# The decay rows of the first pair of heads: written in place by two engines, or transferred

## The chip, the cores and the metric

The kernel runs on one core of a Trainium2 chip. The metric is the device time of one execution in microseconds (us). Each core has five engines: TensorE (PE, with its weight loads shown apart as PEld), VectorE (DVE), ScalarE (ACT), GpSimd (POOL) and SyncE (SP, which here issues the transfers).

## The reference

The program is causal attention with a decay, for 8 batches of 8 heads (576 tokens, head size 64), and behind it a gated mixing network over the tokens. Cut to what matters:

```python
scores = scale * np.matmul(q, k.transpose(0, 1, 3, 2))
log_f = np.log(np.clip(f, 0.0001, 1.0))
cum = np.cumsum(log_f, axis=-1)
decay = cum[:, :, :, None] - cum[:, :, None, :]
scores = np.where(causal, -1000000000.0, scores + decay)
attn = softmax(scores)                       # 1e-9 added to the sum
x = heads side by side of np.matmul(attn, v)
h = np.maximum(x @ w_in, 0.0)
u, v = h[..., :d_ff // 2], h[..., d_ff // 2:]
gated = u * (w_spatial @ normalised(v) + b_spatial)
out = gated @ w_out
```

## The kernel before

The heads are worked in 32 pairs. `attention` runs over the four pairs of a batch, `moe` over the batches; an outer loop takes steps of both in turn by fixed costs, and a scheduler then orders each engine's instructions for the whole program. A call `after(i, mark)` asks it to put `i` behind an earlier instruction; it adds no wait on the chip.

For a head, `scores` makes four tiles of 128 queries (128, 256, 384 and 512 keys) and `scores_tail` the last 64 queries of both heads. TensorE multiplies queries by keys into PSUM (three buffers at the start), VectorE adds the mask `zm` and takes the row extremum (L287, L308), ScalarE takes the exponential and its sum (L289, L313), POOL scales by the reciprocal sum (L297, L320). `tt[0]`, `tt[1]` and `tl` hold the results. Then come transposes (L343, L356) and the product with the values (`attend`).

The decay is part of the score product. An operand tile `tf` has 66 partitions: 64 of the head's size and two rows of decay. Its first 640 columns are queries, the last 576 keys. In the key columns the two rows are cum and 8; in the query columns they are -8 and cum; in query columns that belong to the other head of the pair they are 0. Their product adds 8 times the difference of the cumulative sums, and VectorE's step scales by -0.125.

`decay_rows` makes these rows once for all 64 heads, one head to a partition, in `r0`: constants by `decay_consts` (POOL memsets L82 and L83, VectorE memsets L85), the gates `f` by a transfer (L95), clamp (L100), Ln (L101), the running sum (L103), then `queries_rows` copies the sums into the query columns (L89 on VectorE, L91 on ScalarE). The one-element exponential in L102 makes ScalarE load its table early. `prep` loads a head's operand for the first four pairs: one transfer of queries and keys (L241) and one of the two decay rows from `r0` (L242). Later pairs read their rows from `rows_d` in memory, which `split_rows` fills: `rt` holds the sums in two parts (ScalarE casts L110, L89, L91 and a POOL subtraction L111), and one transfer stores it (L113).

While the first pair's operands are made, TensorE runs 30 products of zeros (`zm`), so that its clock is at full speed when the scores begin.

Weights come in 64-bit form by transfers at L135 and are converted by `conv64` (ScalarE L144, VectorE L145 to L151, POOL L153 and L155), in turn with the attention of the first batches. SP issues all loads from one queue, in order; an issue that waits holds those behind it.

Of the kernel before, what the change touches and what calls it, by code (L numbers as in the profile page):

```python
# [8 lines left out]
F32 = mybir.dt.float32  # L9
F32R = mybir.dt.float32r  # L10
BF16 = mybir.dt.bfloat16
U32 = mybir.dt.uint32
AF = mybir.ActivationFunctionType
ALU = mybir.AluOpType
# [8 lines left out]
S = 576  # L23
D = 64
NB = 4
TL = 512
# [3 lines left out]
QK = 640 + S  # L30
# [3 lines left out]
def f32(ap):  # L34
    return ap.bitcast(F32)
# [3 lines left out]
def attn_gmlp_kernel(ctx: ExitStack, tc: tile.TileContext, qk, v, f, w_in, w_sp, b_sp, w_out, out):  # L39
# [11 lines left out]
    cst = ctx.enter_context(tc.tile_pool(name="cst", bufs=1))  # L51
    wk = ctx.enter_context(tc.tile_pool(name="wk", bufs=1))
# [4 lines left out]
    V, A, G, T, SY = nc.vector, nc.scalar, nc.gpsimd, nc.tensor, nc.sync  # L57


    ident = cst.tile([128, 128], F32, name="ident")  # L60
    make_identity(nc, ident)

    zm = cst.tile([128, 928], BF16, name="zm")
    G.memset(zm, 0.0)
# [6 lines left out]
    lnc = cst.tile([128, 3], F32, name="lnc")  # L71
# [7 lines left out]

    def decay_consts(r, rows):  # L80
        r = f32(r)
        G.memset(r[:, 0:rows, 0:640], -8.0)  # L82
        G.memset(r[:, rows:2 * rows, 640:QK], 8.0)  # L83
        for p0, h in ((0, 0), (32, 1)):
            V.memset(r[p0:p0 + 32, :, S - 64 * h:640 - 64 * h], 0.0)  # L85

    def queries_rows(r, rows, copy, copy_tail):
        r_ = f32(r)
        copy(r[:, rows:2 * rows, 0:TL], r_[:, 0:rows, 640:640 + TL])  # L89
        for p0, h in ((0, 0), (32, 1)):  # L90
            copy_tail(r[p0:p0 + 32, rows:2 * rows, TL + 64 * h:S + 64 * h], r_[p0:p0 + 32, 0:rows, 640 + TL:QK])  # L91

    def decay_rows():
        ft = wk.tile([64, S], F32, name="ft", tag="vt")
        SY.dma_start(out=ft, in_=f)  # L95
        ones = wk.tile([64, S], F32, name="ones", tag="xl", bufs=5)
        V.memset(ones, 1.0)
        r0 = cst.tile([64, 2, QK], F32, name="r0", tag="el")
        decay_consts(r0[:], 1)
        V.tensor_scalar(out=ft, in0=ft, scalar1=1.0e-4, scalar2=1.0, op0=ALU.max, op1=ALU.min)  # L100
        A.activation(ft, ft, AF.Ln)  # L101
        A.activation(lnc[0:1, 2:3], ft[0:1, 0:1], AF.Exp)  # L102
        V.tensor_tensor_scan(out=r0[:, 0, 640:QK], data0=ones, data1=ft, initial=0.0, op0=ALU.mult, op1=ALU.add)  # L103
        queries_rows(r0[:], 1, V.tensor_copy, A.copy)
        return r0

    def split_rows(ws, r0):
        rt = ws.tile([64, 4, QK], F32R, name="rt", bufs=1)
        decay_consts(rt[:], 2)
        A.copy(rt[:, 0, 640:QK], r0[:, 0, 640:QK])  # L110
        G.tensor_tensor(out=rt[:, 1, 640:QK], in0=r0[:, 0, 640:QK], in1=f32(rt[:, 0, 640:QK]), op=ALU.subtract)  # L111
        queries_rows(rt[:], 2, A.copy, A.copy)
        after(SY.dma_start(out=rows_d[:], in_=f32(rt[:])), ("exp", 0, 1, 0))  # L113

    last = {}
# [11 lines left out]
    def after(i, mark):  # L127
        if mark in last:
            tc.add_manual_dep(i.ins, last[mark].ins.name, mybir.DependencyInfo(
                mybir.DependencyClass.NoSync, mybir.DependencyReason.DATA), reason="order")  # L130
# [71 lines left out]
                    SY.dma_start(out=f32(sptb[64 + r:65 + r, :]), in_=f32(bs[r][:]))  # L202
            yield 1000

    tt = [cst.tile([128, 1280], F32, name=f"tt{h}") for h in range(2)]
    tl = cst.tile([128, 640], F32, name="tl")
    G.memset(tl[:, S:640], 0.0)
    ET = {"f": cst.tile([128, 2, 1600], F32, name="ef", tag="eh")}
# [3 lines left out]
    def mm(o, l, r, st, sp):  # L212
        last['mm'] = T.matmul(o, l, r, start=st, stop=sp)  # L213
        return last['mm']
# [6 lines left out]
    vts, tab, parts, r0s = {}, {}, {}, []  # L221
# [14 lines left out]
    def prep(P, h):  # L236

        p = slice(64 * h, 64 * h + 64)
        if P < NQ:
            ta = wk.tile([66, QK], F32, name="tf", tag="ta" if P % 2 == 0 else "tb", bufs=2)  # L240
            after(SY.dma_start(out=ta[0:64, :], in_=qk[P, p, :]), ("dma", 0, 1))  # L241
            last['dma', P, h] = SY.dma_start(out=ta[64:66, :], in_=r0s[0][32 * h + P:32 * h + P + 1])  # L242
            tab[P, h] = (ta,)
            return
        hi, lo = parts[P]
        ta = wk.tile([128, QK], F32R, name="ta", tag="ta", bufs=2)
        tb = wk.tile([128, QK], F32R, name="tb", tag="tb", bufs=2)
        SY.dma_start(out=f32(ta[0:64, :]), in_=hi[p, :])
        SY.dma_start(out=f32(ta[64:128, 0:640]), in_=lo[p, 0:640])
        SY.dma_start(out=f32(ta[64:128, 640:QK]), in_=hi[p, 640:QK])  # L250
        SY.dma_start(out=f32(tb[0:64, 0:640]), in_=hi[p, 0:640])
        SY.dma_start(out=f32(tb[0:64, 640:QK]), in_=lo[p, 640:QK])
        after(SY.dma_start(out=f32(tb[64:68, :]), in_=rows_v[:, P, h, :]), ("exp", P - 1, 0, 0))
        tab[P, h] = (ta, tb)
# [144 lines left out]
    def attention(b, ws=None):  # L399
        for P in range(b * PPB, (b + 1) * PPB):  # L400
            if P == 0:
                r0s.append(decay_rows())
                for h in range(2):
                    prep(0, h)

                warm = ps_a.tile([128, 512], F32, name="x0")
                for _ in range(30):
                    mm(warm, zm[:, 0:128], zm[:, 0:512], True, True)
                yield from scores(0, 0)
                yield from scores_tail(0)  # L410
                yield from scores(0, 1)
                for _ in range(6):
                    after(T.matmul(warm, zm[:, 0:128], zm[:, 0:512], start=True, stop=True), 'mm')
            nxt = P + 1 < NPAIR
            prep_v(P)
            if nxt:
                prep(P + 1, 0)
                prep(P + 1, 1)
            if P == 0:
                split_rows(ws, r0s[0])  # L420
            yield from transposes(P, 0)
            if nxt:
                yield from scores(P + 1, 0)
            yield from transposes_tail(P)
            if P + 2 < NPAIR:
                split(P + 2)
            if nxt:
                yield from scores_tail(P + 1)
            xh = wk.tile([128, 640], F32R, name="xh", tag="xh", bufs=5)
            xl = wk.tile([128, S], F32R, name="xl", tag="xl", bufs=5)  # L430
            yield from attend(P, 0, xh, xl)
            yield from transposes(P, 1)
            if nxt:
                yield from scores(P + 1, 1)
            yield from attend(P, 1, xh, xl)
            A.copy(xh[:, S:640], f32(xl[:, TL:S]))
            xs[P] = (xh, xl)
# [210 lines left out]
```

## Time and profile before

| what | value |
|---|---|
| median of 3 runs | 809.53 us (809.02 to 810.04) |
| profiled execution | 809.19 us |
| its span, first to last instruction | 807.4 us |
| mean granted TensorE clock | 0.991 |
| PE, DVE, ACT, POOL busy | 97%, 68%, 66%, 59% of the span |

A row of the timeline has the start and duration in us, the engine, the line, the operation, what it writes and reads, and in brackets the idle time before it and what ended that. The chain of work that ended last follows the end back through whatever released each step. SPq rows are issues of transfers, not their duration; landings have no rows.

### The profile page before, as it was taken

The page shows a single profiled execution, that of the slowest core. Times are in us where ns is not written, and L with a number is a line of the kernel's source. Part 1 is how long each engine was busy: PE and PEld are TensorE (multiplying, and loading weights), DVE is VectorE, ACT ScalarE, POOL GpSimd, SP SyncE. Part 2 cuts the span into 40 slices and gives each one's busy share as a digit, 9 for nine tenths or more (in the row PEclk, how much of TensorE's full clock was granted, in tenths as well). Part 3 has the DMA queues.
Part 4 walks back from the last instruction along what each step waited for, and adds up shares of the span by engine and source line. Part 5 has one row for each costly group of instructions (what it writes and reads, how often), then busy time and mean ns, then how long its engine had stood idle before and what let it go on. Part 6 is the DMA issues. An engine that isn't in the chain of part 4 may idle for free.

```text
span 807.4 us, 15507 instructions
## 1 busy us (share of the span) xinstructions
PE 786.1 (97%) x4989; PEld 704.5 (87%) x4990; DVE 550.9 (68%) x1658; ACT 536.2 (66%) x1416; POOL 479.0 (59%) x660
## 2 busy tenths in 40 slices
PE   9998989999999999999999999999999999999997
PEld 4676768998999879998899989999899988999996
DVE  5989696766756568675867668666777757665421
ACT  6768557666767578675877668577777757664431
POOL 5879697565646566554766647456675537543241
PEclk9999999999999999999999999999999999999999
DMA  6866535564465553566545644555553655330001
GB/s 175 257 228 157 150 91 140 133 166 123 97 143 134 145 153 83 130 163 162 134 115 139 161 119 120 143 136 142 145 143 106 156 148 133 74 78 14 27 1 66
DMA packets 40179, 103.49 MB, mean 128 GB/s; under 512 B 6833, under 2 KB 6833, under 8 KB 40034
## 3 DMA queue, kind: packets, MB, share of 16 engines
q1 hardware_dynamic: 39778, 101.98, 48.8%
q8 instruction: 40, 0.66, 0.3%
q10 hardware_dynamic: 320, 0.52, 0.2%
q14 instruction: 41, 0.34, 0.1%
HBM read 39.41 MB, written 10.68 MB: 62 GB/s over the span
## 4 chain that ended last, share of the span: by engine, by line
PE 85%; POOL 4%; DVE 4%; DMA 2%; ACT 2%; issue 1%; SPq 0%; POOLq 0%; ACTq 0%; DVEq 0%
PE ps L213 46%; PE sc L213 15%; PE x L213 12%; PE tp L343 7%; PE tp L213 2%; PE tp L356 2%; DMA w<-in_dram 2%; POOL tt L297 1%; DVE tt L287 1%; DVE vx L481 1%; POOL w L153 1%; DMA out_dram<-o 1%; POOL win L155 1%; ACT tt L289 0%; DVE wa L151 0%
## 5 line engine op out<-in xcount | busy, mean ns | idle before, releaser
L297 POOL TENSOR_SCALAR tt<-tt,sm 128x128 f32<-128x128 f32 (+3 forms) x256 | 141.2, 570 | 116.5 <-DVE sm L293 67.8
L287 DVE CUSTOM_DVE_ANT_0 tt<-sc,zm 128x128 f32<-128x128 f32 (+3 forms) x256 | 122.4, 486 | 109.1 <-PE tp L343 77.8
L332 ACT CAST eh<-tp 128x512 fp32r<-128x512 f32 (+1 forms) x270 | 111.4, 425 | 82.1 <-PE tp L343 51.3
L289 ACT ACTIVATE tt<-tt,nm 128x128 f32<-128x128 f32 (+3 forms) x256 | 144.4, 565 | 24.8 <-DVE nm L287 23.6
L333 DVE TENSOR_TENSOR el<-tp,eh 128x512 fp32r<-128x512 f32 (+1 forms) x270 | 127.4, 485 | 20.2 <-ACT eh L332 17.9
L343 PE MATMUL tp<-ident,tt 128*128 128x128 f32 x640 | 113.3, 279 | 4.0 <-POOL tt L297 1.8
L213 PE MATMUL sc<-ta 128*128 128x128 f32 (+1 forms) x336 | 108.8, 329 | 2.3 <-DVE nm L287 1.9
L213 PE MATMUL sc<-tb 68*128 68x128 f32 (+1 forms) x336 | 105.7, 319 | 0.0
L213 PE MATMUL x<-eh,vt 128*128 128x320 f32 (+4 forms) x378 | 103.4, 285 | 1.8 <-POOL vt L264 1.8
L213 PE MATMUL ps<-xh,win 128*128 128x256 f32 (+1 forms) x464 | 99.5, 303 | 2.1 <-DVE vx L475 2.1
L529 POOL TENSOR_TENSOR gl<-u,gh 128x256 fp32r<-128x256 f32 x64 | 47.2, 738 | 81.2 <-ACT gh L528 81.0
L213 PE MATMUL ps<-win,xh 128*128 128x512 f32 x296 | 91.9, 403 | 0.5 <-ACT o L554 0.4
L233 POOL TENSOR_TENSOR lo<-raw,hi 128x640 fp32r<-128x640 f32 (+1 forms) x56 | 83.7, 1515 | 14.6 <-ACT hi L231 14.4
L213 PE MATMUL x<-el,vt 128*128 128x256 f32 x324 | 91.3, 305 | 0.0
L343 PEld LDWEIGHTS tp<-ident,tt 128*128 128x128 f32 x640 | 77.1, 142 | 16.1 <-POOL tt L297 4.2
L213 PEld LDWEIGHTS ps<-xh,win 128*128 128x128 f32 x464 | 76.3, 191 | 3.5 <-DVE vx L475 1.9
L213 PEld LDWEIGHTS x<-eh,vt 128*128 128x128 f32 x378 | 71.4, 189 | 4.5 <-POOL vt L264 2.7
L213 PE MATMUL ps<-sph,vnh 128*128 128x256 f32 (+1 forms) x240 | 73.3, 306 | 0.2 <-ACT o L554 0.2
L391 ACT CAST xh<-x 64x256 fp32r<-64x256 f32 (+1 forms) x128 | 50.1, 394 | 33.6 <-PE x L213 31.4
L213 PE MATMUL ps<-sph,vnl 128*128 128x256 f32 (+1 forms) x240 | 71.7, 299 | 0.0
L213 PEld LDWEIGHTS sc<-ta 128*128 128x128 f32 x336 | 64.4, 192 | 7.9 <-DVE nm L287 3.2
L213 PE MATMUL ps<-spl,vnh 128*128 128x256 f32 (+1 forms) x240 | 71.2, 297 | 0.0
(173 smaller groups left out, 1916.6 us busy)
## 6 DMA issues: line engine op xcount, KB each, us to landing
raw<-in_dram SPq DMA_DIRECT2D x28, 608.0 KB
ta<-hi SPq DMA_DIRECT2D x56, 304.0 KB
vraw<-in_dram SPq DMA_DIRECT2D x32, 320.0 KB
ta<-lo SPq DMA_DIRECT2D x56, 160.0 KB
tb<-hi SPq DMA_DIRECT2D x56, 160.0 KB
out_dram<-o SPq DMA_DIRECT2D x32, 256.0 KB
ta<-hi SPq DMA_DIRECT2D x56, 144.0 KB
tb<-lo SPq DMA_DIRECT2D x56, 144.0 KB
```

The lines of the kernel that those rows point to most:

```text
L153: G.tensor_tensor(out=wf, in0=wf, in1=af, op=ALU.add)
L213: last['mm'] = T.matmul(o, l, r, start=st, stop=sp)
L233: G.tensor_tensor(out=lo[:, c], in0=raw[:, c], in1=f32(hi[:, c]), op=ALU.subtract)
L287: V.tensor_tensor_reduce(out=t, in0=sc[:, 0:n], in1=zm[:, 640 - n:640], scale=-0.125, scalar=3.0e38, op0=ALU.add, op1=ALU.min, accum_out=n ...
L289: last["exp"] = last["exp", P, h, i] = A.activation(t, t, AF.Exp, bias=nm[:, i:i + 1], scale=-1.0, accum_out=se[:, i, 0:1])
L297: G.tensor_scalar(out=t, in0=t, scalar1=sm[:, i:i + 1], scalar2=1.0, op0=ALU.mult, op1=ALU.mult)
L332: A.copy(h_ap, ps)
L333: V.tensor_tensor(out=l_ap, in0=ps, in1=f32(h_ap), op=ALU.subtract)
L343: T.transpose(out=tp[:, (i - c) * 128:(i - c + 1) * 128], in_=tt[h][:, TOFF[i] + 128 * c:TOFF[i] + 128 * c + 128], identity=ident)
L356: T.transpose(out=tp[:, j * 128:(j + 1) * 128], in_=tl[:, c * 128:(c + 1) * 128], identity=ident)
L391: last[P, h] = A.copy(hi, ps[m0:m0 + 64, 0:n])
L529: G.tensor_tensor(out=gl[j][:, 0:256], in0=g[:, 0:256], in1=f32(gh[j][:, 0:256]), op=ALU.subtract)
```

## The change

For the first pair alone, the two decay rows of each head are no longer transferred from `r0`. The gates are read a second time (`ft` has 128 partitions now), so that partitions 64 to 95 all hold the gates of head 0 of the pair and 96 to 127 those of head 1. The running sums of a head therefore stand in partitions 64 and 65 or 96 and 97 too, and `first_rows` writes the operand's two partitions from them: each row is the sums times a 0 or 1 taken from the identity matrix, plus or minus an 8 or 0 taken from `id8`. ScalarE writes the key columns, VectorE the query columns; small VectorE memsets write the zeros.

Around it, `queries_rows` for `r0` is called after the first four score tiles. The casts for `rt` get a mark behind the first head's last exponential, and the constants' memsets one behind the last of the new VectorE operations. The warming products are 18 and read zeros that VectorE writes into `tt[1]`. The mark `("dma", 0, 1)`, which the loads of other pairs and of the first weights are put behind, is now a VectorE instruction.

```diff
+    tt = [cst.tile([128, 1280], F32, name=f"tt{h}") for h in range(2)]
+    V.memset(tt[1][:, 0:320], 0.0)
+    zz = tt[1][:, 0:320].bitcast(BF16)
...
+    id8 = cst.tile([128, 64], F32, name="id8")
+    V.tensor_scalar(out=id8, in0=ident[:, 64:128], scalar1=8.0, scalar2=1.0, op0=ALU.mult, op1=ALU.mult)
...
-        G.memset(r[:, 0:rows, 0:640], -8.0)
-        G.memset(r[:, rows:2 * rows, 640:QK], 8.0)
+        after(G.memset(r[:, 0:rows, 0:640], -8.0), ("dma", 0, 1))
+        after(G.memset(r[:, rows:2 * rows, 640:QK], 8.0), ("dma", 0, 1))
...
-        ft = wk.tile([64, S], F32, name="ft", tag="vt")
-        SY.dma_start(out=ft, in_=f)
+        ft = wk.tile([128, S], F32, name="ft", tag="vt")
+        SY.dma_start(out=ft[64:128, :], in_=bass.AP(tensor=f.tensor, offset=f.offset, ap=[[32 * S, 2], [0, 32], [1, S]]))
+        SY.dma_start(out=ft[0:64, :], in_=f)
...
-        queries_rows(r0[:], 1, V.tensor_copy, A.copy)
         return r0
+
+    def first_rows(r, h):
+        g = slice(64 + 32 * h, 66 + 32 * h)
+        c = r0s[0][g, 0, 640:QK]
+        k, q = 32 * h, 32 * h + 1
+        ik, iq = (ident[g, 64 + n:65 + n] for n in (k, q))
+        bk, bq = (id8[g, n:n + 1] for n in (k, q))
+        A.activation(r[:, 640:QK], c, AF.Identity, bias=bq, scale=ik)
+        for a, n, o in ((0, S, 0),) if h == 0 else ((0, TL, 0), (TL, S - TL, 64)):
+            i = V.tensor_scalar(out=r[:, a + o:a + o + n], in0=c[:, a:a + n], scalar1=iq, scalar2=bk, op0=ALU.mult, op1=ALU.subtract)
+        return i
...
-        A.copy(rt[:, 0, 640:QK], r0[:, 0, 640:QK])
-        G.tensor_tensor(out=rt[:, 1, 640:QK], in0=r0[:, 0, 640:QK], in1=f32(rt[:, 0, 640:QK]), op=ALU.subtract)
+        after(A.copy(rt[:, 0, 640:QK], r0[0:64, 0, 640:QK]), ("exp", 0, 0, 3))
+        G.tensor_tensor(out=rt[:, 1, 640:QK], in0=r0[0:64, 0, 640:QK], in1=f32(rt[:, 0, 640:QK]), op=ALU.subtract)
...
-            last['dma', P, h] = SY.dma_start(out=ta[64:66, :], in_=r0s[0][32 * h + P:32 * h + P + 1])
+            if P == 0:
+                V.memset(ta[64:66, S - 64 * h:640 - 64 * h], 0.0)
+                last['dma', P, h] = first_rows(ta[64:66], h)
+            else:
+                last['dma', P, h] = SY.dma_start(out=ta[64:66, :], in_=r0s[0][32 * h + P:32 * h + P + 1])
...
-                for _ in range(30):
-                    mm(warm, zm[:, 0:128], zm[:, 0:512], True, True)
+                for _ in range(18):
+                    mm(warm, zz[:, 0:128], zz[:, 128:640], True, True)
                 yield from scores(0, 0)
+                queries_rows(r0s[0][0:64], 1, V.tensor_copy, A.copy)
```

Lines of the changed kernel stand higher by 6 to 22; L153 there is L135 here, L258 is L241, L263 is L242, L308 is L287 and L318 is L297.

SP's queue at the start, before (`w` are the raw weights, `vraw` the values; a number behind a name tells buffers apart):

```order
L95 DMA ft<-in_dram 64x576
L241 DMA tf<-in_dram 64x1216 x2
L242 DMA tf<-r_122 2x1x1216 x2
L135 DMA w_201<-in_dram 128x1024
L135 DMA w_203<-in_dram 128x1024
L258 DMA vraw<-in_dram 128x640
L241 DMA tf<-in_dram 64x1216
L242 DMA tf<-r_122 2x1x1216
```

and now:

```order
L101 DMA ft<-in_dram 64x1x576
L102 DMA ft<-in_dram 64x576
L258 DMA tf<-in_dram 64x1216 x2
L153 DMA w_199<-in_dram 128x1024
L153 DMA w_201<-in_dram 128x1024
L279 DMA vraw<-in_dram 128x640
L258 DMA tf<-in_dram 64x1216
L263 DMA tf<-r_126 2x1x1216
L153 DMA w_203<-in_dram 128x1024
```

The two transfers of the first pair's rows are gone; the first one that needs the sums is the second pair's, behind two weight loads, the values and an operand.

VectorE's queue up to the first score tile, before (the scan L103 is printed as SCALAR_TENSOR_TENSOR, the score step as ISA):

```order
L97 MEMSET ones 64x576
L100 TENSOR_SCALAR ft<-ft 64x576
L85 MEMSET r_122 32x2x64 x2
L103 SCALAR_TENSOR_TENSOR r_122<-ones,ft 64x576
L89 COPY r_122<-r_122 64x512
L85 MEMSET rt 32x4x64 x2
L287 ISA tt_96,nm<-sc,zm 128x128
```

and now:

```order
L104 MEMSET ones 128x576
L260 MEMSET tf 2x64 x2
L67 TENSOR_SCALAR id_74<-ident 128x64
L108 TENSOR_SCALAR fl<-ft 128x576
L91 MEMSET r_126 32x2x64 x2
L111 SCALAR_TENSOR_TENSOR r_126<-ones,fl 128x576
L122 TENSOR_SCALAR tf<-r_126,ident,id_74 2x576
L122 TENSOR_SCALAR tf<-r_126,ident,id_74 2x512
L122 TENSOR_SCALAR tf<-r_126,ident,id_74 2x64
L95 COPY r_126<-r_126 64x512
L91 MEMSET rt 32x4x64 x2
L308 ISA tt_66,nm<-sc,zm 128x128
```

Three operations of the first pair stand between the scan and the copy; the copy and the memsets of `rt` keep their place ahead of the first tile.

POOL's queue around the first scalings, before (`zm` by AFFINE_SELECT is the mask):

```order
L82 MEMSET rt 64x2x640
L83 MEMSET rt 64x2x576
L65 AFFINE_SELECT zm<-zm 128x128
L68 AFFINE_SELECT zm<-zm 64x64 x2
L111 TENSOR_TENSOR rt<-r_122,rt 64x576
L297 TENSOR_SCALAR tt_96<-tt_96,sm 128x128
```

and now:

```order
L71 AFFINE_SELECT zm<-zm 128x128
L74 AFFINE_SELECT zm<-zm 64x64 x2
L88 MEMSET rt 64x2x640
L89 MEMSET rt 64x2x576
L318 TENSOR_SCALAR tt_66<-tt_66,sm 128x128
L318 TENSOR_SCALAR tt_66<-tt_66,sm 128x256
L318 TENSOR_SCALAR tt_66<-tt_66,sm 128x384
L318 TENSOR_SCALAR tt_66<-tt_66,sm 128x512
L129 TENSOR_TENSOR rt<-r_126,rt 64x576
L341 TENSOR_SCALAR tl<-tl,sm 128x576
```

The mask comes ahead of the memsets of `rt`, and the subtraction for `rt` behind the four scalings.

More of the change, by code (lines that the diff above doesn't have):

```diff
@@ L93, in decay_rows @@
     def decay_rows():
-        ft = wk.tile([64, S], F32, name="ft", tag="vt")
-        SY.dma_start(out=ft, in_=f)
-        ones = wk.tile([64, S], F32, name="ones", tag="xl", bufs=5)
+        ft = wk.tile([128, S], F32, name="ft", tag="vt")
+        SY.dma_start(out=ft[64:128, :], in_=bass.AP(tensor=f.tensor, offset=f.offset, ap=[[32 * S, 2], [0, 32], [1, S]]))
+        SY.dma_start(out=ft[0:64, :], in_=f)
+        ones = wk.tile([128, S], F32, name="ones", tag="xl", bufs=5)
         V.memset(ones, 1.0)
[L98 to L103, printed above, removed]
-        queries_rows(r0[:], 1, V.tensor_copy, A.copy)
-        return r0
+        r0 = cst.tile([128, 2, QK], F32, name="r0", tag="el")
+        decay_consts(r0[0:64], 1)
+        fl = wk.tile([128, S], F32, name="fl", tag="xh", bufs=5)
+        V.tensor_scalar(out=fl, in0=ft, scalar1=1.0e-4, scalar2=1.0, op0=ALU.max, op1=ALU.min)
+        A.activation(fl, fl, AF.Ln)
+        A.activation(lnc[0:1, 2:3], fl[0:1, 0:1], AF.Exp)
+        V.tensor_tensor_scan(out=r0[:, 0, 640:QK], data0=ones, data1=fl, initial=0.0, op0=ALU.mult, op1=ALU.add)
+        return r0
+    def first_rows(r, h):
[8 more added lines that the diff above has]
+        return i
     def split_rows(ws, r0):
@@ L203, in load_late @@
             yield 1000
-    tt = [cst.tile([128, 1280], F32, name=f"tt{h}") for h in range(2)]
     tl = cst.tile([128, 640], F32, name="tl")
@@ L412, in attention @@
                 for _ in range(6):
-                    after(T.matmul(warm, zm[:, 0:128], zm[:, 0:512], start=True, stop=True), 'mm')
+                    after(T.matmul(warm, zm[:, 640:768], zm[:, 0:512], start=True, stop=True), 'mm')
             nxt = P + 1 < NPAIR
```

## The prediction

> **What bounds the kernel now.** I read the page first, then the table of busy time by stretch, then the chain and the timeline of the first 26 us, since the change touches only the start.
>
> ```profile
> span 807.4 us, 15507 instructions
> PE 786.1 (97%) x4989; PEld 704.5 (87%) x4990; DVE 550.9 (68%) x1658; ACT 536.2 (66%) x1416; POOL 479.0 (59%) x660
> ```
> ```profile
> 20.00:40.00 20.00, 19.18 (x93) 13.19 (x92) 18.99 (x57) 14.68 (x41) 16.51 (x19) 1.00 0.83 254
> 40.00:60.00 20.00, 19.59 (x89) 14.06 (x87) 17.52 (x55) 13.70 (x36) 15.99 (x16) 0.91 0.65 230
> 140.00:160.00 20.00, 20.00 (x159) 19.57 (x158) 14.47 (x48) 13.63 (x38) 11.78 (x16) 1.00 0.58 144
> ```
>
> The columns of the stretches are PE, PEld, DVE, ACT, POOL, then granted clock, DMA share and GB/s. From 140 us on PE is the bound. From 20 to 60 us DVE is busy 18.99 and 17.52 of 20 us, so there PE and VectorE run close together. No row shows PE waiting for a particular absolute time there: whatever starts all engines earlier should carry through, unless the new order loses it again. The start is this:
>
> ```profile
> 1.79 9.32 PE x L213 x30
> 11.11 4.75 PE sc L213 x20
> ```
> ```profile
> 0.72 0.59 SPq L95 DMA_DIRECT2D ft<-in_dram  x1
> 0.90 0.54 DVE L97 MEMSET ones<- 64x576 f32 x1 [0.90 <-PEq L634]
> 3.53 0.89 DVE L100 TENSOR_SCALAR ft<-ft 64x576 f32<-64x576 f32 x1 [2.10 <-DMA ft<-in_dram]
> 4.46 0.68 ACT L101 ACTIVATE ft<-ft 64x576 f32<-64x576 f32 x1 [2.46 <-DVE ft L100]
> 5.18 1.35 DVE L103 TENSOR_TENSOR_SCAN r<-ones,ft 64x576 f32<-64x576 f32 x1 [0.38 <-ACT ft L101]
> ...
> 6.46 0.20 ACT L102 ACTIVATE lnc<-ft 1x1 f32<-1x1 f32 x1
> 6.56 0.50 DVE L89 COPY r<-r 64x512 f32<-64x512 f32 x1
> 6.57 0.51 ACT L91 COPY r<-r 32x64 f32<-32x64 f32 x2
> 6.88 0.15 PEld L213 LDWEIGHTS <-zm 128*128 128x128 bf16 x1 [0.28 <-issue]
> 7.05 0.63 DVE L85 MEMSET rt<- 32x256 f32 x2
> 7.10 0.67 ACT L110 CAST rt<-r 64x576 fp32r<-64x576 f32 x1
> 7.16 1.39 SPq L242 DMA_DIRECT2D tf<-r  x2
> 7.28 3.33 PEld L213 LDWEIGHTS <-zm 128*128 128x128 bf16 x16 [0.24 <-issue]
> 7.85 1.41 POOL L111 TENSOR_TENSOR rt<-r,rt 64x576 fp32r<-64x576 f32 x1 [0.40 <-ACT rt L110]
> 8.59 0.87 SPq L135 DMA_DIRECT2D w<-in_dram  x2
> 9.29 1.04 ACT L89 CAST rt<-rt 64x1024 fp32r<-64x1024 f32 x1 [1.52 <-POOL rt L111]
> ...
> 10.24 0.60 ACT L91 CAST rt<-rt 32x128 fp32r<-32x128 f32 x2
> ```
>
> The chain is PE alone until 15.9 us: 30 warming products, 1.79 to 11.11 us, then the scores. Beside it runs the decay path: gates in at 3.53, clamp, Ln, scan, copies, and at 7.16 the transfer of the rows into the operand. Its landing has no row. The gates' transfer took 3.53 - 0.72 = 2.8 us from issue to use; the same for the rows gives 7.16 + 2.8 = 10.0 us. So the products cover the transfer and outlast it by about 1.1 us.
>
> **The change part by part.** (a) *Gates read twice.* One more transfer on SP, issued first, and the clamp waits for both: one issue, +0.59 us, so the clamp starts at 4.1 us. If the two land as one, it is nothing; if the second only starts when the first has landed, it is 2.8 us, for which no row speaks. I take 0.59, what the row of one issue shows. Both operands' loads (L241) and all behind them on SP are issued 0.59 us later, well before they are used. Twice the partitions should cost nothing: VectorE's copy of 64x512 took 0.50 us (6.56), its operation on 128x512 at 15.80, below, 0.42. Clamp, Ln and scan keep 0.89, 0.68 and 1.35: scan ends at 6.53 + 0.59 = 7.12 us.
>
> (b) *The engines write the rows.* ScalarE: two Identity operations on 2x576, nearest row the 64x576 cast, 0.67 us each: 7.2 to 7.9 for head 0, to 8.55 for head 1. VectorE: pieces of 576, 512 and 64 columns. Between the 0.42 us of a 128x512 operation at 15.80 (below) and the 0.89 us of the clamp, which ran beside POOL's memsets, I take the low end, 0.5, 0.45 and 0.15, since POOL has nothing to do from 7.85 - 0.40 = 7.45 us on: 7.15 to 8.25; with the high end (0.89, 0.79 and 0.3), to 9.1. Two small memsets and the scaled identity go into VectorE's 2.10 us wait and cost nothing while the gates land after 3 us. PE can therefore start the scores at about 7.95 us instead of 11.11.
>
> (c) *18 warming products for 30*, started by a VectorE memset of 320 columns (320/576 of 0.54 = 0.3 us, from 0.90) instead of at 1.79: start 1.25 us. Before, the weight loads came one every 0.4 us up to the row at 6.88, the rest in one group of 16 in 3.33 us, 0.208 each; 30 products and the first two loads of the scores make that 13 or 14 slow ones, (7.28 - 1.79)/13 = 0.42 us each. So 13 x 0.42 + 5 x 0.208 = 6.5 us, end 7.8: it just covers the rows. PE's gain is 11.11 - 7.95 = 3.1 us.
>
> (d) *What is late next: VectorE.* The copies of the other pairs' query rows (L89, 0.50) and the memsets of rt (0.63) stand in its queue before the first score tile, as before, but now directly in front of it: 8.25 + 1.13 = 9.4 us.
>
> ```profile
> 11.49 0.29 DVE L287 CUSTOM_DVE_ANT_0 tt<-sc,zm 128x128 f32<-128x128 f32 x1 [3.80 <-PE sc L213]
> ...
> 13.31 0.69 DVE L287 CUSTOM_DVE_ANT_0 tt<-sc,zm 128x512 f32<-128x512 f32 x1 [0.29 <-PE sc L213]
> ...
> 14.67 0.19 ACT L289 ACTIVATION_READ_ACCUMULATOR tt<-tt,nm 128x1 f32 x1
> ...
> 15.36 0.52 DVE L308 CUSTOM_DVE_ANT_0 tl<-sc,zm,nm 128x288 f32<-128x288 f32 x1
> 15.47 2.49 POOL L297 TENSOR_SCALAR tt<-tt,sm 128x128 f32<-128x128 f32 x4 [6.21 <-ACT wa L144]
> ...
> 15.80 0.42 DVE L145 TENSOR_SCALAR wa<-wa 128x512 f32<-128x512 f32 x1
> ```
>
> Before, VectorE waited 3.80 us for that tile; now PE waits. It has three score buffers, so it stands at the fourth tile until the first is read out. First tile: 11.49 - 9.45 = 2.0 us earlier (1.2 with the long operations of (b), 2.6 if the gates' second read cost nothing). ScalarE's four exponentials follow that tile, and ended 14.86 - 11.49 = 3.4 us after it; they hold the sums, the tail tile at 15.36 and POOL's scaling at 15.47. Those come 2.0 us earlier too: the other 1.1 us of PE's head start become waiting.
>
> (e) *Work moved behind the start.* POOL's subtraction for rt (1.41) moves from its idle time at 7.85 behind the first four scalings, and ScalarE's casts for rt (0.67 + 1.04 + 0.60 = 2.3 us) between the exponentials.
>
> ```profile
> 18.78 0.75 POOL L320 TENSOR_SCALAR tl<-tl,sm 128x576 f32<-128x576 f32 x1 [0.82 <-ACT tt L289]
> ...
> 20.61 1.27 POOL L153 TENSOR_TENSOR w<-w,wa 128x512 f32<-128x512 f32 x1 [1.09 <-DVE wa L151]
> ...
> 28.95 0.78 ACT L313 ACTIVATE tl<-tl,nm 128x576 f32<-128x576 f32 x1 [2.34 <-DVE nm L308]
> ```
>
> POOL idles 0.82 + 1.09 = 1.91 us around 18 to 20 us, which holds the 1.41; ScalarE idles 2.34 us before 28.95. I take 0 and keep 1.3 for the range, by the next rows:
>
> ```profile
> 17.86 0.68 DVE L148 SCALAR_TENSOR_TENSOR w<-w,wa 128x512 uint32<-128x512 uint32 x1
> ...
> 24.21 1.27 POOL L155 TENSOR_TENSOR win<-w,win 128x512 fp32r<-128x512 f32 x1
> ...
> 24.42 1.62 DVE L148 SCALAR_TENSOR_TENSOR w<-w,wa 128x512 uint32<-128x512 uint32 x1
> ```
>
> The same VectorE instruction takes 0.68 us with POOL idle and 1.62 with POOL's subtraction beside it, ending 0.56 us after that. Moved, the 1.41 us fall on 15.9 to 17.3 us, where this very instruction (17.86 - 2.0 = 15.86) will stand. The Trainium skill, "SBUF — State Buffer", section "SBUF: two separate sides", says that the port pair shared by the two is an exclusive lock: who starts first holds it for its whole instruction. The 1.62 us agree with it; by it the sum would lose up to a whole 1.41 us and the time would be 807.5 + 1.41 = 808.9.
>
> (f) *SP.* The first two weight loads, paced by SP's order behind the rows' transfers, were issued at 8.59 us; now nothing waits ahead of them and they go at about 3.1, the second pair's rows from 9.1. The transfer of rt to memory goes later, with (e); its first reader is the fifth pair. Earlier weights help only where conversions wait for data; no wait shows that, so 0.
>
> **Sum.** -2.0 us on the profiled execution's 809.19 gives 807.2; its median stands at 809.53, against which it is 807.5. I forecast 807.5; its own range 806.8 to 808.3, by the ends of (a) and (b) (1.2 and 2.6) about 2.0.
>
> **Rivals.** *1. Given back by 35 us.* The lock above, or ScalarE's 2.3 us between exponentials, costs 0.7 to 1.4 of the 2.0 (half of the 1.41, or all). For it: VectorE 18.99 of 20 us busy in 20 to 40. Against: POOL's 1.91 us idle. 808.2 to 808.9, no measurable change (0.2%, 1.6 us, is about what a measurement of this kernel can tell).
>
> *2. A second long stop, slower.* The order changes on all engines up to about 120 us.
>
> ```profile
> 110.22 1.52 DVE L150 TENSOR_SCALAR wa<-w 128x512 uint32<-128x512 uint32 x1
> ...
> 112.25 0.81 PE L213 MATMUL x<-ef,vraw 128*128 128x320 f32 x2 [2.13 <-DVE xl L392]
> ```
> ```profile
> 110.00:115.00 5.00, 2.87 (x10) 2.15 (x10) 5.00 (x14) 2.92 (x9) 4.47 (x5) 0.80 0.01 2
> 115.00:120.00 5.00, 5.00 (x30) 4.35 (x29) 4.94 (x10) 2.02 (x5) 5.00 (x6) 0.85 0.33 71
> ```
>
> There VectorE's subtraction (L392) stood behind a slow weight conversion, PE stopped 2.13 us and the clock was 0.80 and 0.85 for 10 us: 2.13 + 1.75 = 3.9 us. A second such place gives 807.5 + 3.9 = 811.4; it decides from a cost of 3.7 us on. Against: nothing in the start forces it, and the place could as well vanish.
>
> *3. Such a stop vanishes, or the earlier weights shorten 20 to 80 us:* 2 us more, 805.5.
>
> *4. The scores don't start earlier,* because the second gate read lands 2.8 us late: the first tile of VectorE then comes at 9.45 - 0.59 + 2.8 = 11.7 us for 11.49, so 809.7 at worst, no change. Against: L241's two transfers went out 0.6 us apart in the same way.
>
> **How the numbers follow.** Forecast 0.45, rival 1 0.27, rival 2 0.10, rival 3 0.12, rival 4 0.06. Faster 0.45 + 0.12 = 0.57, same 0.27 + 0.06 = 0.33, slower 0.10. The range 805.2 to 810.0 leaves out rival 2 and the better half of rival 3.
>
> **What would show it.** First score product at 8 us (if 10 or later, (a) or (b) is wrong), 18 products ending near 7.8, first VectorE tile at 9.4 with PE waiting for it, the first scaling on POOL at 13.4, weights issued near 3 us. Rival 1 shows as a conversion on VectorE of 1.3 us or more at 16 us. The prediction is wrong if PE's idle time or its low clock between 20 and 140 us changes by more than 1.5 us.

## The result: 1.35% slower

The changed kernel took 820.06 us (median of 4 runs, 819.05 to 820.77); the kernel before, beside it on the same chip, 809.27 us (4 runs, 807.91 to 810.04). The ratio is 1.0135, with a 95% interval of 1.0122 to 1.0147. The forecast was 807.5 us.

The profile of the changed kernel, first the page's span and busy times, then its row of the granted clock in 40 slices:

```profile
span 817.9 us, 15473 instructions
PE 793.2 (97%) x4977; PEld 708.1 (87%) x4978; DVE 558.4 (68%) x1665; ACT 537.0 (66%) x1418; POOL 480.4 (59%) x660
...
PEclk7898997999999999999999999999999999999999
```

PE is busy 7.1 us longer than before (793.2 for 786.1) though it runs 12 warming products fewer: some of the work ran at a low clock. The timeline of the changed kernel shows where that begins:

```profile
0.72 0.72 SPq L101 DMA_DIRECT2D ft<-in_dram  x1
1.24 6.88 PE L230 MATMUL x<-tt 128*128 128x512 bf16 x18 [1.24 <-DVE tt L61]
1.50 0.55 SPq L102 DMA_DIRECT2D ft<-in_dram  x1
7.89 0.46 DVE L108 TENSOR_SCALAR fl<-ft 128x576 f32<-128x576 f32 x1 [5.60 <-DMA ft<-in_dram]
8.39 0.68 ACT L109 ACTIVATE fl<-fl 128x576 f32<-128x576 f32 x1 [6.39 <-DVE fl L108]
9.11 1.36 DVE L111 TENSOR_TENSOR_SCAN r<-ones,fl 128x576 f32<-128x576 f32 x1 [0.40 <-ACT fl L109]
10.61 1.74 ACT L120 ACTIVATE tf<-r,id,ident 2x576 f32<-2x576 f32 x2
11.52 9.75 PE L230 MATMUL sc<-tf 66*128 66x128 f32 x20 [3.40 <-ACT tf L120]
12.97 0.29 DVE L308 CUSTOM_DVE_ANT_0 tt<-sc,zm 128x128 f32<-128x128 f32 x1
```

The clamp (L108) waits 5.60 us for the gates and starts at 7.89 us, where the kernel before had them at 3.53. The warming products end at 8.12 us, PE stands still for 3.40 us, and the first 20 score products take 9.75 us, for 4.75 before. The start of the chain of work that ended last, cut to two of its pieces (start, duration), leads to the gates:

```profile
1.50 6.29 DMA ft<-in_dram
...
11.52 9.75 PE sc L230 x20
```

Its DMA row begins at 1.50 us, where the plain read of the gates (L102) is issued: that read, which stands behind the additional one (L101), released the clamp.

Busy time by stretch of the changed kernel (PE, PEld, DVE, ACT, POOL, granted clock, DMA share, GB/s). By the clock record that the trace keeps, the clock is at half from 10.4 us, within the standstill, to 27.5 us:

```profile
10.00:15.00 5.00, 3.48 (x7) 2.27 (x8) 3.95 (x13) 3.76 (x10) 0.00 (x0) 0.54 0.90 290
15.00:20.00 5.00, 5.00 (x11) 3.24 (x10) 1.47 (x8) 2.64 (x6) 0.92 (x3) 0.50 0.50 153
20.00:25.00 5.00, 5.00 (x12) 2.63 (x12) 4.20 (x14) 3.32 (x9) 3.33 (x4) 0.50 0.27 64
25.00:30.00 5.00, 4.78 (x19) 3.02 (x19) 3.51 (x12) 3.92 (x13) 1.49 (x3) 0.75 0.76 208
```

To follow the loss through the span, I compare the start of each pair's last cast on ScalarE (L436, and L458 in the changed kernel) with the same cast of the kernel before, which stands at 39.08 us for pair 0, 172.22 for pair 6 and 760.13 for the last pair. The changed kernel is 8.32 us late at pair 0, 10.31 at pair 6 and 10.49 at the last one. So about 8.3 us are lost before 47 us, 2 us net between there and 182 us, and 0.2 after that. In between the figure swings (5.24 at pair 1, 13.62 at pair 3), as it does in every kernel with the new order, so single pairs there are not read.

### The profile page after: what moved, and what is told of

It reads as the page before. It is cut to its first block, busy times and chain, and to the rows that moved or that the text cites. A ratio compares the mean times of both kernels' runs of the same rounds, so it can differ in the third digit from the quotient of the medians.

```text
span 817.9 us, 15473 instructions
## 1 busy us (share of the span) xinstructions
PE 793.2 (97%) x4977; PEld 708.1 (87%) x4978; DVE 558.4 (68%) x1665; ACT 537.0 (66%) x1418; POOL 480.4 (59%) x660
## 4 chain that ended last, share of the span: by engine, by line
PE 84%; DVE 5%; POOL 5%; ACT 2%; DMA 2%; issue 2%; SPq 1%; POOLq 0%; ACTq 0%; DVEq 0%
PE ps L230 44%; PE sc L230 16%; PE x L230 11%; PE tp L364 8%; PE tp L230 2%; PE tp L377 2%; POOL tt L318 2%; DVE tt L308 1%; POOL w L171 1%; POOL win L173 1%; DMA ft<-in_dram 1%; DVE vx L503 1%; POOL lo L250 1%; DVE el L354 1%; DVE w L166 1%
## 5 line engine op out<-in xcount | busy, mean ns | idle before, releaser
L318 POOL TENSOR_SCALAR tt<-tt,sm 128x128 f32<-128x128 f32 (+3 forms) x256 | 141.9, 571 | 106.7 <-DVE sm L314 83.8
L308 DVE CUSTOM_DVE_ANT_0 tt<-sc,zm 128x128 f32<-128x128 f32 (+3 forms) x256 | 122.8, 486 | 98.2 <-PE tp L364 68.6
```

The lines of the kernel that those rows point to most:

```text
L308: V.tensor_tensor_reduce(out=t, in0=sc[:, 0:n], in1=zm[:, 640 - n:640], scale=-0.125, scalar=3.0e38, op0=ALU.add, op1=ALU.min, accum_out=n ...
L318: G.tensor_scalar(out=t, in0=t, scalar1=sm[:, i:i + 1], scalar2=1.0, op0=ALU.mult, op1=ALU.mult)
```

## Experiments

The theory after the first comparison: the additional gate read makes the gates late because its access pattern has an outermost dimension of 2, and the standstill this makes halves the clock. Each run below is compared with runs of the kernel before on the same chip.

### Is it the pattern of the read, or that rows are repeated?

*distinct*: the same shape of read, but from 63 different rows (one of them twice). The diff is cut to the argument that changes.

```diff
-ap=[[32 * S, 2], [0, 32], [1, S]]
+ap=[[31 * S, 2], [S, 32], [1, S]]
```

> The changed kernel with one edit: the second gate read takes 64 different rows in two overlapping groups of 32 (outer dimension still 2) instead of two rows 32 times each, so the copied sums are those of other heads. All instruction orders are those of the changed kernel. If the read is slow because its outermost dimension is 2 and it so runs on few transfer engines, the clamp still starts near 7.9 us and the time stays at 820 (819 to 821). If it is slow because the same row is fetched 32 times, the clamp starts near 4.5 us, the scores near 8 us, and the time falls by 8 us or more, to 812 or less.

It took 822.08 us, ratio 1.0157 (1.0142 to 1.0172). The clamp of this kernel in its timeline:

```profile
9.40 0.46 DVE L108 TENSOR_SCALAR fl<-ft 128x576 f32<-128x576 f32 x1 [7.11 <-DMA ft<-in_dram]
```

With one row read twice, and none 32 times, it comes 1.5 us later still, and the time lies above the 819 to 821 expected. Repeated rows are not the cause.

*wide*: the read as two transfers, one for each head, each of 32 partitions with 32 as the outermost dimension.

```diff
-SY.dma_start(out=ft[64:128, :], in_=bass.AP(..., ap=[[32 * S, 2], [0, 32], [1, S]]))
+for h in range(2):
+    SY.dma_start(out=ft[64 + 32 * h:96 + 32 * h, :], in_=bass.AP(..., ap=[[0, 32], [1, S]]))
```

> The changed kernel with the second gate read issued as two transfers, one for each head, whose outermost dimension is 32 rather than 2; the rows are still fetched 32 times each, the data are the same. Few engines as the cause: gates by 5 us at the latest (one more issue of 0.6 us), scores from about 8.7 us without a long stop of PE, clock at full, 20 to 40 us as before the change: 806 to 810. Repeated rows as the cause: gates still near 7.9 us, 820.

It took 812.91 us, ratio 1.0045 (1.0028 to 1.0063). From its timeline:

```profile
4.57 0.46 DVE L109 TENSOR_SCALAR fl<-ft 128x576 f32<-128x576 f32 x1 [0.49 <-DMA ft<-in_dram]
8.20 5.02 PE L231 MATMUL sc<-tf 66*128 66x128 f32 x20 [0.28 <-ACT tf L121]
```

The clamp has the same bytes 3.3 us earlier, PE stops for 0.28 us only, and pair 0 is 1.57 us ahead of the kernel before. At pair 6 it is 3.28 us late and at the end 1.74, and the time is above the 806 to 810 expected: there is a second loss, behind the start.

This kernel differs from the changed one in the dimension, in the number of transfers and in places of the instruction order. *flat* has one transfer for the additional read, and the instruction order of the changed kernel on every engine (diff cut as above):

```diff
-ap=[[32 * S, 2], [0, 32], [1, S]]
+ap=[[S, 64], [1, S]]
```

> As the changed kernel, but the second gate read's source is written with one outer dimension of 64 rows, [[S, 64], [1, S]], for [[32 * S, 2], [0, 32], [1, S]]: still one transfer of 64 x 576 into the same partitions. It reads the gates of all 64 heads, so the first pair's decay is computed from other heads' gates; the order of the instructions on every engine is that of the changed kernel. Theory (the outermost dimension of 2 makes the transfer slow, not that there is one transfer more): clamp at 3.6 to 4.6 us for 7.89, scores at 7.3 to 8.3 behind the 18 products with a stop under 0.5 us, the clock full from 10 us on, pair 0 about 8.3 us earlier than in the changed kernel and 1.6 ahead of the kernel before; what then stays at the end is the cost of this order alone, by the decomposition 2 to 4 us, so 810 to 813. Rival (one wide transfer instead of two is what helped in the kernel with two): clamp at 6 us or later, half the clock after 10 us, 816 to 820.

It took 811.15 us (12 runs), ratio 1.0033 (1.0021 to 1.0046). From its timeline:

```profile
1.24 6.43 PE L230 MATMUL x<-tt 128*128 128x512 bf16 x18 [1.24 <-DVE tt L61]
4.41 0.47 DVE L108 TENSOR_SCALAR fl<-ft 128x576 f32<-128x576 f32 x1 [2.11 <-DMA ft<-in_dram]
8.05 1.57 PE L230 MATMUL sc<-tf 66*128 66x128 f32 x6 [0.39 <-ACT tf L120]
9.51 0.29 DVE L308 CUSTOM_DVE_ANT_0 tt<-sc,zm 128x128 f32<-128x128 f32 x1
13.19 2.39 POOL L318 TENSOR_SCALAR tt<-tt,sm 128x128 f32<-128x128 f32 x4 [6.00 <-ACT wa L162]
15.48 0.68 DVE L166 SCALAR_TENSOR_TENSOR w<-w,wa 128x512 uint32<-128x512 uint32 x1
15.55 1.88 POOL L129 TENSOR_TENSOR rt<-r,rt 64x576 fp32r<-64x576 f32 x1
```

The clamp starts at 4.41 us: the dimension makes the read late, not the additional transfer. Against *distinct*, which reads its 64 rows as 2 x 32, the clamp starts 5.0 us earlier. And since the order is that of the changed kernel, the difference of the two is what this one pattern costs: each against the kernel before on its own chip, 10.8 - 2.5 = 8.3 us by the medians.

How the read was carried stands in the traces too, in the times at which the completion of each transfer is counted; they are no rows of the views. In *flat* the additional read is counted sixteen times, from 2.92 to 3.36 us. In the changed kernel it is counted once at 1.82 us, before its first row is under way, and then twice more, at 6.92 and 7.09; in *distinct* at 1.82, 8.72 and 8.84. The plain read behind it is counted sixteen times in all three: in *flat* the last is at 4.31 us; in *distinct* fourteen come by 4.33 and two at 9.00 and 9.30; in the changed kernel fourteen come by 6.80 and two at 7.65 and 7.79, and there the clamp is released. The Trainium skill, "DMA: Bandwidth & Descriptors", section "Rules for kernel authors", states a rule that fits: an outermost dimension smaller than 16, its example a leading zero-stride broadcast, confines the whole transfer to at most that many engines. The counts agree: two late ones for the read of 2 x 32, sixteen for that of 64, and two late parts of the plain read queued behind the former.

*before_dbl*: the kernel before, with the doubled read alone. The rows are still transferred, and the upper 64 partitions are used by nothing but the clamp, which waits for both reads.

```diff
-ft = wk.tile([64, S], F32, name="ft", tag="vt")
+ft = wk.tile([128, S], F32, name="ft", tag="vt")
+SY.dma_start(out=ft[64:128, :], in_=bass.AP(..., ap=[[32 * S, 2], [0, 32], [1, S]]))
```

> The kernel before with the doubled gate read alone: ft gets 128 partitions and the same two transfers as in the change, the clamp works on all of them and so waits for both, and nothing else is used of the copies. The order of all other instructions is that of before. If the read with outer dimension 2 is what delays the start, the clamp comes at 7.5 to 8 us for 3.5, the transferred rows land near 13.5 us, PE stands still 2 to 2.5 us after its 30 products, and the time is 2 us (811) to 8 us (817) longer, by whether the clock halves. If the read is harmless by itself, no change.

It took 818.80 us, ratio 1.0129 (1.0113 to 1.0144): the read alone, in the order of the kernel before, gives nearly the whole loss, and more than the 811 to 817 expected. From its timeline:

```profile
8.06 0.46 DVE L101 TENSOR_SCALAR ft<-ft 128x576 f32<-128x576 f32 x1 [6.62 <-DMA ft<-in_dram]
14.69 2.90 PE L214 MATMUL sc<-tf 66*128 66x128 f32 x6 [4.34 <-DMA tf<-r]
```

The stop is 4.34 us for the 2 to 2.5 expected. About 0.8 us of it is a side effect of this edit: ScalarE's first table load, 1.28 us long and at 0.71 us in the kernel before, starts here only when the gates are there (8.03 us), and Ln behind it at 9.32, 0.8 us after the clamp's end. Pair 0 is 9.77 us late and the last pair 9.64: with the old order nothing more is lost after the start.

### What did the standstill cost?

*warm36*: the changed kernel with 36 warming products; the gates stay late, but PE doesn't stand still.

```diff
-for _ in range(18):
+for _ in range(36):
```

> The changed kernel with 36 warming products for 18; the gates still land late, at 7.9 us. If the loss is PE's 3.4 us of standing still and the half clock that follows it until 26 us, the products end near 11.6 us, the scores start there at full clock and the first score product of the second pair comes near 20 us for 27.3: 812 to 813, with about 2 us left from later places. If the late start alone costs and the clock is only a symptom, 818 or more.

It took 816.05 us, ratio 1.0089 (1.0074 to 1.0104). From its timeline:

```profile
1.24 10.44 PE L230 MATMUL x<-tt 128*128 128x512 bf16 x36 [1.24 <-DVE tt L61]
8.04 0.46 DVE L108 TENSOR_SCALAR fl<-ft 128x576 f32<-128x576 f32 x1 [5.74 <-DMA ft<-in_dram]
11.67 1.57 PE L230 MATMUL sc<-tf 66*128 66x128 f32 x6
```

The scores start as late as in the changed kernel (11.67 for 11.52) at a clock of 1.00, and pair 0 is 2.41 us late for 8.32. At pair 0, half the clock after the standstill cost 5.9 us; the late start itself costs 2.41 + 1.20 = 3.6 us against *flat*, which is what its clamp is later (8.04 - 4.41). The time was put too low, 812 to 813: the last pair of this kernel is 8.33 us late, so it loses another 5.9 us behind pair 0, where the changed kernel loses 2.2. Its order differs a little from the changed kernel's behind the start (on SP's queue from the tenth issue on), so what the standstill is worth at the end is less certain: 10.8 - 6.9 = 3.9 us by the medians.

*before18* and *before24*: the kernel before with fewer warming products, 18 and 24 for 30. They ask how much of the start could be had without the engines writing the rows.

```diff
-for _ in range(30):
+for _ in range(18):     # before24: range(24)
```

> The kernel before with 18 warming products for 30 and nothing else; the order of all other instructions is unchanged. The rows are transferred as before. The products end near 8.3 us. If the transferred rows land near 10.0 us and 1.7 us of standing still is short enough for the clock, the scores start at 10 and the time is 808.4 (1 us faster). If a stop of 1.7 us already halves the clock, it is slower by 3 to 8 us: 812 to 817.

> The kernel before with 24 warming products for 30, order otherwise unchanged. With 18 the transferred rows landed at 9.07 us and PE stood still 1.8 us. 13 slow and 11 fast products end at 1.79 + 5.5 + 2.3 = 9.6 us, just behind the landing: no stop, scores 1.5 us earlier than before, so 807.5 to 808 where the start carries through; no change if it is given back.

They took 808.52 us, ratio 0.9996 (0.9985 to 1.0006), and 808.32 us, ratio 0.9994 (0.9986 to 1.0003): no measurable change. The timeline of *before18*, then that of *before24*, at the first scores:

```profile
9.07 7.31 PE L213 MATMUL sc<-tf 66*128 66x128 f32 x20 [1.79 <-DMA tf<-r]
```
```profile
9.29 4.99 PE L213 MATMUL sc<-tf 66*128 66x128 f32 x20 [0.31 <-DMA tf<-r]
```

The transferred rows, issued at 6.93 us, are there at 9.07: 2.1 us, not the 2.8 that the prediction took from the gates. So the 30 products outlasted the transfer by 2 us, and a shorter row of products gives most of the earlier start that the change wanted: *before24* is 1.58 us ahead at pair 0, as far as *wide*. It keeps about 1.1 of that from pair 15 on, and its median is 0.4 us below that of the kernel before, within the noise. So even in the old order the earlier start carries through only in part in this execution. The profiled execution of *before18* took 812.1 us, the longest of its ten (the others 807.9 to 810.9); its stop of 1.79 us was followed by half the clock, and the same 20 products took 7.31 us:

```profile
15.00:20.00 5.00, 5.00 (x13) 2.70 (x12) 3.46 (x13) 2.56 (x8) 1.92 (x4) 0.50 1.06 238
```

### Where does the rest go, between 100 and 185 us?

Waits of PE of at least 0.9 us between 100 and 185 us, as the timeline has them; first the kernel before, then the changed one, then *flat*:

```profile
112.25 0.81 PE L213 MATMUL x<-ef,vraw 128*128 128x320 f32 x2 [2.13 <-DVE xl L392]
122.34 0.56 PE L213 MATMUL ps<-xh,win 128*128 128x320 f32 x2 [1.67 <-DVE vx L475]
```
```profile
118.13 0.45 PE L230 MATMUL sc<-ta 128*128 128x384 f32 x1 [1.14 <-DVE nm L308]
122.09 0.33 PE L364 MATMUL tp<-ident,tt 128*128 128x128 f32 x1 [2.68 <-DVE ef L349]
132.99 0.41 PE L364 MATMUL tp<-ident,tt 128*128 128x128 f32 x2 [1.92 <-DVE el L354]
135.65 0.61 PE L230 MATMUL sc<-ta 128*128 128x288 f32 x1 [0.98 <-DVE nm L308]
```
```profile
109.13 0.44 PE L230 MATMUL sc<-ta 128*128 128x384 f32 x1 [1.14 <-DVE nm L308]
110.72 1.26 POOL L171 TENSOR_TENSOR w<-w,wa 128x512 f32<-128x512 f32 x1
110.80 1.74 DVE L166 SCALAR_TENSOR_TENSOR w<-w,wa 128x512 uint32<-128x512 uint32 x1 [1.16 <-POOL wo L173]
112.46 0.55 DVE L349 COPY ef<-tp 128x384 f32<-128x384 f32 x1
113.06 0.48 PE L364 MATMUL tp<-ident,tt 128*128 128x128 f32 x1 [2.65 <-DVE ef L349]
123.95 0.41 PE L364 MATMUL tp<-ident,tt 128*128 128x128 f32 x2 [1.68 <-DVE el L354]
126.61 0.61 PE L230 MATMUL sc<-ta 128*128 128x288 f32 x1 [1.48 <-DVE nm L308]
```

The old order has two such stops, 3.80 us together; the new one has four, at the same instructions whenever the start was, 6.72 us in the changed kernel and 6.95 in *flat*. The rows around the longest stop, in *flat*, show how it comes about: VectorE waits 1.16 us for POOL's last reader of a conversion buffer (L173), then its conversion (L166) runs 1.74 us beside POOL's addition (L171), which began 0.08 us ahead of it, and the copy that PE's next product needs (L349) stands behind both. The clock is lower too, as the stretches of 40 us show, before and then *flat*:

```profile
100.00:140.00 40.00, 34.93 (x200) 30.09 (x199) 32.47 (x84) 25.31 (x64) 35.08 (x39) 0.91 0.46 118
```
```profile
100.00:140.00 40.00, 32.69 (x161) 26.10 (x160) 34.83 (x90) 24.12 (x60) 34.57 (x39) 0.83 0.51 128
```

Five runs change the order or that wait. *wide_wu3* gives the late weights' conversions three buffers instead of two; *wide_late51* puts the last conversions behind an exponential of the second head instead of the first; *wide_nomark* takes the mark off the first cast for `rt`, *wide_nomark_wu3* does that with three buffers, and *flat_early* takes back the calls behind part (e) of the prediction (no mark, and the copies of the other pairs' rows called ahead of the warming products).

```diff
# wide_wu3, wide_nomark_wu3
-tc.tile_pool(name="wu", bufs=2, reuse_waits="tile")
+tc.tile_pool(name="wu", bufs=3, reuse_waits="tile")
# wide_late51
-wo[n] = conv64(f"wo{n}", wu, ("exp", 5, 0, n))
+wo[n] = conv64(f"wo{n}", wu, ("exp", 5, 1, n))
# wide_nomark, wide_nomark_wu3, flat_early
-after(A.copy(rt[:, 0, 640:QK], r0[0:64, 0, 640:QK]), ("exp", 0, 0, 3))
+A.copy(rt[:, 0, 640:QK], r0[0:64, 0, 640:QK])
# flat_early also: queries_rows(...) from behind scores(0, 0) to ahead of the products
```

> The kernel with the gates read in two wide transfers, and three buffers instead of two for the last weights' conversion, so that VectorE's step that overwrites a buffer need not wait for POOL's last reader. If the stop of 2.7 us at 112 us, which stands behind that step, and the other stops up to 130 us are what keeps the early start from paying, PE's waits between 100 and 185 us fall from 8 to 5 us or less and the time from 812.9 to 809 or less. If the order as a whole is at fault, another stop takes its place: 811 to 814.

> The kernel with the gates read in two wide transfers, and the last weights' conversions put behind the exponentials of the sixth pair's second head instead of its first, so that they meet other work. Stops from the order: their sum between 100 and 185 us changes by 2 us or more in either direction, and the time with it, 809 to 816, while pairs 0 to 3 end as in the wide kernel within 0.5 us. If the loss comes from something else, 812.9 as before.

> The kernel with the gates read in two wide transfers, without the mark that puts the first cast for rt behind the first head's last exponential, so that this work is placed as the scheduler likes (as before the change). The start stays: pair 0 ends 1.6 us earlier than in the kernel before. If the order between 100 and 185 us decides the rest, PE's waits there and the time differ from the wide kernel's by 1.5 us or more in either direction (808 to 816); if rt's work between the exponentials is itself the price, pairs 0 to 2 end 0.5 to 1 us earlier still and the time is 811.5 to 812.5.

> The same with three buffers for the last weights' conversion, as a try for a version that beats both: start 1.6 us earlier, and the stop behind VectorE's wait for POOL gone. 807 to 809 if no other stop takes its place, 810 to 812 if the order at 100 to 185 us again makes one.

> As the kernel with one flat gate read of 64 rows, and part (e) of the prediction undone: the casts for rt have no mark behind the first exponentials and the copies of the other pairs' query rows are called before the warming products, as in the kernel before, so the work on rt is no longer moved behind the start. Theory (the loss at 100 to 185 us comes from the order of the whole program, which differs again, not from the moved work itself): same start, scores near 8 us, VectorE stops of PE at 100 to 185 us still there in some form, end 809 to 813, no measurable gain on the kernel before. Rival (the moved work on ScalarE, VectorE and POOL is what costs): PE idle in 15 to 60 us and at 100 to 185 us as in the kernel before (1.07 and 4.99 us), and the gain of 1.6 us at pair 0 stays to the end: 807.

| kernel | median us | ratio (95%) | pair 0 | pair 6 | last pair |
|---|---|---|---|---|---|
| wide | 812.91 | 1.0045 (1.0028 to 1.0063) | -1.57 | +3.28 | +1.74 |
| flat | 811.15 | 1.0033 (1.0021 to 1.0046) | -1.20 | +1.87 | +3.11 |
| wide_wu3 | 810.73 | 1.0029 (1.0012 to 1.0046) | -1.72 | +0.70 | +1.10 |
| wide_late51 | 819.03 | 1.0133 (1.0119 to 1.0147) | -1.73 | +10.85 | +9.73 |
| wide_nomark | 809.96 | 1.0023 (1.0006 to 1.0039) | +4.58 | +6.31 | +5.53 |
| wide_nomark_wu3 | 811.17 | 1.0039 (1.0014 to 1.0064) | +0.42 | +1.98 | +2.21 |
| flat_early | 814.61 | 1.0082 (1.0067 to 1.0098) | -0.08 | +5.44 | +4.13 |

The last three columns are us against the kernel before, from one profiled execution each, so they need not end at the difference of the medians. A third buffer shortens PE's idle time at 100 to 185 us from 7.99 to 6.31 us (before: 4.99), between the two cases that its text had set apart. Its interval overlaps that of *wide*, and beside *wide_nomark* a third buffer gives no gain, so it isn't shown to help. A mark moved by one head ends 8 us later than *wide* (+9.73 for +1.74) after the same start, above the 809 to 816 expected. PE's idle time there is only 0.7 us longer, where a change of 2 us or more was expected; what differs is the clock, 0.84 for 0.94 over these 85 us, which is 8.5 us. First *wide*, then *wide_late51*:

```profile
100.00:185.00 85.00, 76.80 (x482) 67.50 (x481) 62.43 (x179) 54.24 (x143) 60.12 (x75) 0.94 0.49 126
```
```profile
100.00:185.00 85.00, 75.92 (x427) 65.21 (x426) 58.08 (x156) 51.33 (x130) 49.38 (x60) 0.84 0.42 107
```

*wide_nomark*'s median is below *wide*'s, with overlapping intervals, and *flat_early* is clearly slower than *flat*. Neither settles what the work on `rt` costs. In *flat_early* it isn't out of the way as in the kernel before: ScalarE makes the casts at 11.50 and 12.46 us, ahead of the first head's fourth exponential, which starts at 13.08 for 11.76 in *flat*, and POOL's first scaling comes at 14.73 for 13.19. What *flat_early* does show is that the four stops don't hang on part (e): they stand at the same instructions, 1.16, 2.67, 1.91 and 0.93 us long. None of these kernels beats the kernel before. In the profiled execution of *wide_nomark*, 814.8 us and the longest of its ten (the next 811.6), a stop for the second pair's rows fell into the start:

```profile
18.28 0.52 PE L231 MATMUL sc<-tf 66*128 66x128 f32 x2 [2.08 <-DMA tf<-r]
```
```profile
20.00:25.00 5.00, 5.00 (x13) 3.07 (x12) 4.11 (x10) 2.57 (x7) 4.16 (x6) 0.50 0.96 286
```

What stays open: which places of the new order make the four stops, out of the many that moved. The runs show that seven kernels with a new order, whose scores all start between 7.9 and 8.2 us, reach the last pair 1.1 to 9.7 us later than the kernel before, and the size of it was not told from the edit: two came out above the range expected. No run isolates one moved instruction, so that the order is the cause is shown for *wide_late51* against *wide* (one mark), and argued for the rest.

## Why the prediction was wrong

**The step that failed: (a), the gates read twice.** It took one issue, 0.59 us, and set aside 2.8 us, "for which no row speaks". The read cost 7.89 - 3.53 = 4.4 us at the clamp, above both. The working looked at the issue and at the number of partitions, never at how the pattern was written. What it used against rival 4, that the operands' two transfers went out 0.6 us apart, was about issues; the outermost dimension of those is 64. *flat* gives the term with the pattern mended: 4.41 - 3.53 = 0.9 us.

**A missing term: what a standstill of PE does to the clock.** Rival 4 had the right mechanism, the read landing late, and drew from it 809.7 us "at worst", by VectorE's first tile alone. With 18 products ending at 8.12 us, late rows must leave PE idle for as long as they are late, and 3.4 us of it cost 5.9 us more at pair 0, at half the clock. The row of it was in the prediction (2.13 us of stop, then 0.80 and 0.85 of the clock for 10 us), used only for a stop at 112 us. The change had taken away 12 products that would have covered most of this; (c) priced only what they freed.

**Rival 2 came true in kind.** It spoke of a second long stop near 112 us, with a price that gave 811.4 us; with the gates mended, *flat* measures 811.15. That the figures meet is luck: not one stop was added, but four came in place of two, 3.15 us longer together, with a lower clock. The rival was given one chance in ten because "nothing in the start forces it". Yet the order was new on every engine up to 120 us, and all seven kernels that have a new order and the gates in time are slower than the one before, by 0.23 to 1.33%, each with its whole interval above 1. The time lost there is the difference between *flat* at pair 0 and at the end, 1.20 + 3.11 = 4.3 us in its profiled execution.

**The sum as it came out,** at pair 0: -1.2 (what the change gives with the read mended), +3.6 (late gates), +5.9 (half clock) = +8.3 us; then about +2 by the order, less than *flat* loses there. By the medians the loss of 820.06 - 809.27 = 10.8 us is 8.3 for the read and 811.15 - 808.65 = 2.5 for the rest.

**What was taken for granted:** that whatever starts all engines earlier carries through. *before24* is 1.58 us ahead at pair 0 in the old order and no gain can be measured, so a gain of 2.0 us at the end was doubtful even with the read mended and the order unharmed.

**What held.** By *flat*, with the read mended: the first score product at 8.05 us (7.95 predicted), the 18 products ending at 7.67 (7.8), VectorE's first tile at 9.51 (9.4) with PE waiting for it, POOL's first scaling at 13.19 (13.4), the weights issued at 3.27 (3.1). The gain was put at 2.0 us; it is 11.49 - 9.51 = 2.0 at VectorE's first tile and 1.2 to 1.6 at pair 0. That these times meet so closely is partly luck, since errors cancel: the clamp starts at 4.41 us for 4.1 but takes 0.47 for 0.89, VectorE's three pieces take 1.39 for 1.10, ScalarE's two operations 1.74 for 1.34. PE's wait for the first tile is 0.24 us, where 1.1 was foreseen. (Two slips of the working change nothing: the lower end of the range about 2.0 is 806.9, not 806.8, and POOL was not idle beside the whole conversion of 0.68 us, since its scalings ended 0.1 us into it.) Rival 1 did not happen: the conversion at 15.48 us took 0.68 us, and it was POOL's subtraction beside it that grew, to 1.88 from 1.41 us. By the exclusive lock of the Trainium skill, "SBUF — State Buffer", section "SBUF: two separate sides", who starts first holds the ports; here VectorE started first, by 0.07 us, and these rows agree. The prediction had POOL as the holder.

**A term that was sized wrong on the other side:** the transfer of the rows was put at 2.8 us and takes 2.1, so the products outlasted it by 2 us, not 1.1, and most of the earlier start was there for a smaller number in one loop.

## What to carry to other kernels

Read the access pattern of every transfer that the start waits for: with the same 147 KB the clamp could start at 4.4 us for an outermost dimension of 64 and at 7.9 us for 2. Before taking away work that only keeps TensorE busy, price what its standstill costs if the data is late, by a stop and a low clock that the trace already shows. And when an edit at the start reorders the whole program, measure the new order by itself (here with a kernel that has the same order and none of the suspected cost) before the gain of the edit is believed.

## What the runs showed of the hardware

The length of one stop doesn't tell whether the clock halves. After stops of 0.28 to 0.39 us (*wide*, *flat*) and of 1.42 us (*wide_wu3*, at 8.05 us) the clock stayed at 1.00. With 1.79 us (*before18*, its profiled execution), 2.08 us (*wide_nomark*), 3.40 us (the changed kernel) and 4.34 us (*before_dbl*) it fell to 0.50. But it also fell after shorter stops: after 0.96 us in *wide* for 6.8 us, and after 1.03 us in *wide_late51* for 17.1 us, as these rows show, one pair for each:

```profile
64.16 0.82 PE L231 MATMUL x<-ef,vraw 128*128 128x256 f32 x2 [0.96 <-DVE xl L414]
65.00:70.00 5.00, 4.61 (x14) 3.07 (x15) 4.97 (x15) 2.97 (x8) 5.00 (x5) 0.50 1.04 205
```
```profile
133.29 0.33 PE L365 MATMUL tp<-ident,tt 128*128 128x128 f32 x1 [1.03 <-DVE el L355]
135.00:150.00 15.00, 12.82 (x45) 9.75 (x45) 9.51 (x30) 8.81 (x22) 11.50 (x14) 0.50 0.50 118
```

In the clock records of these traces every stretch of half clock, but for the last at the program's end, is 3.41 us long or a whole multiple of it. In the 3.41 us ahead of each, PE stood still for 0.6 to 2.7 us in all. The Trainium skill, "TensorE: Matmul & The Clock Gate", Part 1, speaks of idle windows of about 3.4 us that run freely. The lengths agree with such windows; that PE must stand still for a whole one does not, and the measurement decides here.

A read written as 2 x 32 let the clamp start later with 63 different rows (9.40 us) than with two rows repeated (7.89 and 8.04 us). In both the last to be counted were two parts of the plain read behind it; why they came 1.5 us later with different rows is not shown.
